# A one-core attention and gated-MLP kernel: planned idle products on TensorE, another clock model in the planner, and a table of places

## The chip, the cores and the metric

The kernel runs on one core of one Trainium2 chip. The metric is the device time of one execution in microseconds (us); of several executions the median counts. Engines: TensorE (PE, with its weight loads as PEld), VectorE (DVE), ScalarE (ACT), GpSimd (POOL) and SyncE (SP), which issues the DMAs.

## The reference, cut to what matters

Eight batches of 576 positions pass a sliding-window attention with 8 heads of 64 columns, and then a gated MLP whose gate mixes the positions. All inputs and the output are float32.

```python
scores = scale * np.matmul(q, k.transpose(0, 1, 3, 2))
bias = slopes[:, None, None] * (-np.abs(rel).astype(np.float32))[None, :, :]
mask = (rel >= 0) & (rel < window)                     # window = 128
attn = softmax(np.where(mask, scores + bias[None], -1e9))
x = np.matmul(attn, v)                                 # (8, 576, 8 * 64)
...
h = np.maximum(x @ w_in, 0.0)                          # 512 -> 1024
u, v = (h[..., :d_ff // 2], h[..., d_ff // 2:])
v_n = (v - mu) / np.sqrt(var + 1e-06)
v_s = np.einsum('ts,bsd->btd', w_spatial, v_n) + b_spatial[None, :, None]
gated = u * v_s
return (gated @ w_out).astype(np.float32)
```

## The kernel before

A batch is worked head pair by head pair (four pairs), and each pair in five tiles of one or two blocks of 64 queries (`TILES`). For a pair PE makes the scores in float32 (L635, with L634 writing the masked value), DVE adds the distance bias from a table and takes the row maximum (L667 and L774), ACT takes the exponential with its row sum (L672 and L780), and the rows are scaled (L700 on ACT or L701 on DVE; L814 and L819).

Two paths lead from there to the attention's output. The four pairs of batch 0 and the first pair of batch 1 (`RAW`) stay in float32: PE transposes the probabilities (L713, L715), they are copied out of PSUM (L382), and PE multiplies them with V (L733). All other pairs are split into two f16 halves, transposed by a DMA (L825) and multiplied with V's halves (`vh`, `vl`) on PE (L858). Outputs are split in two f16 halves again (`xt`).

When a batch has its four pairs, the gated MLP follows in units, each of them a group of 12 or 14 full-size products into one of only two PSUM banks named `m`, which ACT or DVE then empties: four units of v and one for the remaining 64 rows (L923, L945) with a layer norm each, eight of u (L974), eight that mix positions (L995, multiplied with u on DVE in L1003), eight of the output (L1023) with a DMA each.

Before all that the weights are prepared on the chip: `w_in` and `w_out` come as float64 words, which ACT and DVE turn into float32 (L398 to L414) and then, scaled by their largest magnitude, into two f16 halves (L430, L441, L456 to L461); the mixing weights are split likewise (`mixing_weights`, L530 and L534).

No order is written down. Every step is handed to a `Plan` with its engine, a weight in ns, a due value and what it reads and writes. `Plan.order` is a list scheduler in virtual time: of the steps that are ready an engine takes the one with the smallest due value. `emit` runs it forward and backward 20 times and keeps the due values of the best pass; `held` then looks for steps in the way of a waiting PE and moves one at a time, up to 100 times. Steps that name two ways (`either`) go to the engine that would end them first. Each engine's instructions are emitted in the order found, and on the chip each engine runs its own in that order. The planner's `order` also models the clock of TensorE, by the time in which PE was planned to be busy. Two kinds of products compute nothing: `warm` (L684) plans 24 groups of 5 products of 192 columns each into a bank of `x` in the first stage, and 2 more ahead of each tile's transposes in 16 tiles of batch 0.

Of the kernel before, what the change touches and what calls it, by code (L numbers as in the profile page):

```python
# [28 lines left out]

FAR = 2.0 ** 38  # L30
# [16 lines left out]
class Plan:  # L47
# [7 lines left out]
    TURN, NEAR = 95, 0  # L55
# [48 lines left out]
    def order(self, links, due, clocked):  # L104
# [9 lines left out]
        low, opened, worked = clocked, 0, 0  # L114
        while events or any(ready.values()):
# [8 lines left out]
            for e, heap in ready.items():  # L124
                if heap and free[e] <= now:
                    _, n, k = heapq.heappop(heap)
                    if e == "PE" and modes[n][head] != mode:
                        same = [x for x in heap if modes[x[1]][head] == mode and x[0] <= due[n] + self.NEAR]
                        if same:
                            heap.remove(min(same))  # L130
                            heapq.heapify(heap)
                            heapq.heappush(heap, (due[n], n, k))
                            _, n, k = min(same)
                    weight = self.ops[n][0][k][1]
                    queued[e] -= weight
                    if e == "SP":
# [35 lines left out]
    def held(self, out, due):  # L172
# [8 lines left out]
        for a, b in zip(line, line[1:]):  # L181
            idle = start[b] - end[a] + self.LAG["PE"]
            if idle < 150:
                continue
            n = b
            for _ in range(12):
                late = [(end[d], d) for d in self.ops[n][2]] + [(start[d], d) for d in self.ops[n][3]]
                if not late:
                    break
# [46 lines left out]
def attn_gmlp_kernel(ctx, tc, qk, v, w_in, w_spT, b_sp, w_out, outT):  # L236
# [3 lines left out]
    nc = tc.nc  # L240
# [908 lines left out]
```

## Time and profile before

| | |
|---|---|
| median of three executions | 577.93 us (576.01 to 578.52) |
| the profiled execution, its own time | 573.51 us |
| its span, first to last instruction | 571.8 us |
| mean granted TensorE clock | 0.991 of 2.4 GHz |
| PE, DVE, ACT busy | 549.9, 465.9, 418.9 us |
| chain that ended last, by engine | PE 68%, DVE 13%, ACT 10%, DMA 6% |

The profile shows one execution. Matmuls are pipelined and each one's record includes its latency, so the pace of PE is read from the starts of groups that follow each other and not from the length of one. An engine's busy share says little by itself: the first tenth of the span loads and prepares weights, the next builds batch 0, and from then on several batches overlap.

### The profile page before, as it was taken

What the parts mean: (1) busy time and instruction counts of PE and PEld (TensorE: products, weight loads), DVE (VectorE), ACT (ScalarE), POOL (GpSimd) and SP (SyncE); (2) the same over time, 40 slices, a digit from 0 to 9 for tenths busy, and PEclk for the clock granted to TensorE, in tenths of its full rate; (3) what the DMA queues carried; (4) which work ended last, traced back from release to release, by engine and by line L of the source; (5) the groups of instructions that cost most, each with busy time, mean ns of one, the idle gap of its engine ahead of it and who ended that gap; (6) DMA issues with size and microseconds to landing.
All of it is one profiled execution on the core that took longest, in us unless ns stands there. A gap on an engine that the chain in (4) does not pass through costs nothing.

```text
span 571.8 us, 17319 instructions
## 1 busy us (share of the span) xinstructions
PE 549.9 (96%) x6657; PEld 396.6 (69%) x6659; DVE 465.9 (81%) x1784; ACT 418.9 (73%) x1368; POOL 58.0 (10%) x121
## 2 busy tenths in 40 slices
PE   5789998999999999999999989999999999999997
PEld 4656555677667766877588765787578757785775
DVE  5889899999998689889987889969997799664541
ACT  6989999999987399589954899638983797443202
POOL 1002122100110102010111002100111010000000
PEclk9989899999999999999999999999999999999999
DMA  8951321599986686569953797737846375371002
GB/s 274 360 228 54 111 93 43 135 168 199 221 188 140 151 190 137 114 196 168 203 107 115 176 196 171 182 96 173 188 86 95 104 138 92 35 136 33 0 11 73
DMA packets 149847, 79.77 MB, mean 140 GB/s; under 512 B 129666, under 2 KB 139906, under 8 KB 149764
## 3 DMA queue, kind: packets, MB, share of 16 engines
q1 hardware_dynamic: 149764, 78.67, 59.6%
q8 instruction: 52, 0.85, 0.6%
q14 instruction: 31, 0.25, 0.1%
HBM read 37.13 MB, written 9.44 MB: 81 GB/s over the span
## 4 chain that ended last, share of the span: by engine, by line
PE 68%; DVE 13%; ACT 10%; DMA 6%; issue 2%; POOL 1%; SPq 0%; ACTq 0%; DVEq 0%; POOLq 0%
PE m L995 17%; PE m L974 13%; PE m L1023 12%; PE m L923 9%; PE s L635 6%; PE x L858 5%; DMA pt<-pq 4%; ACT prob L672 2%; DVE pq L819 2%; PE x L733 2%; ACT pq L814 2%; ACT prob L780 1%; DVE prob L774 1%; DMA out_dram<-o 1%; PE m L945 1%
## 5 line engine op out<-in xcount | busy, mean ns | idle before, releaser
L780 ACT ACTIVATE prob<-prob,stat 64x64 f32<-64x64 f32 (+1 forms) x270 | 113.2, 422 | 12.5 <-DVE stat L774 12.5
L995 PE MATMUL m<-wsp,vn 128*128 128x288 f16 x768 | 114.2, 288 | 0.3 <-ACT u L386 0.2
L1023 PE MATMUL m<-gs,wout 128*128 128x288 f16 x768 | 100.8, 286 | 0.0
L974 PE MATMUL m<-xt,win 128*128 128x288 f16 x768 | 100.4, 286 | 0.4 <-ACT vt L386 0.3
L814 ACT ACTIVATE pq<-prob,stat 64x64 f16<-64x64 f32 (+1 forms) x270 | 94.6, 421 | 6.9 <-ACT prob L780 2.6
L819 DVE SCALAR_TENSOR_TENSOR pq<-prob,stat,pq 64x64 f16<-64x64 f32 (+1 forms) x270 | 92.2, 379 | 3.6 <-ACT pq L814 3.3
L995 PEld LDWEIGHTS <-vn 128*128 128x128 f16 x768 | 74.4, 98 | 21.9 <-issue 2.9
L974 PEld LDWEIGHTS <-win 128*128 128x128 f16 x768 | 74.5, 98 | 21.4 <-issue 1.6
L1023 PEld LDWEIGHTS <-wout 128*128 128x128 f16 x768 | 73.5, 98 | 21.6 <-issue 3.3
L923 PE MATMUL m<-win,xt 128*128 128x512 f16 x384 | 86.4, 379 | 1.9 <-ACT o L1030 1.6
L774 DVE CUSTOM_DVE_ANT_0 prob<-s,tab 64x64 f32<-64x64 f32 (+1 forms) x270 | 73.1, 318 | 8.3 <-PE s L635 8.3
L923 PEld LDWEIGHTS <-xt 128*128 128x128 f16 x384 | 36.6, 98 | 46.3 <-issue 5.4
L635 PE MATMUL s<-qkraw 64*64 64x192 f32 (+2 forms) x1116 | 58.1, 321 | 5.4 <-DMA qkraw<-in_qk_dram 5.1
L1003 DVE TENSOR_TENSOR u<-m,u 128x288 f32<-128x288 f32 x64 | 29.0, 453 | 39.4 <-PE m L995 39.1
L893 POOL TENSOR_TENSOR st<-st,nhalf 128x1 f32<-128x1 f32 (+1 forms) x40 | 30.0, 752 | 304.3 <-DVE st L889 292.4
L386 ACT ACTIVATE u<-m 128x288 f32<-128x288 f32 x57 | 23.2, 407 | 51.2 <-PE m L974 51.2
L1030 ACT ACTIVATE o<-m,am 128x288 f32<-128x288 f32 x42 | 20.8, 496 | 47.3 <-PE m L1023 42.2
L635 PEld LDWEIGHTS s<-qkraw 64*64 64x64 f32 x1116 | 40.7, 135 | 15.7 <-issue 7.2
L780 ACT ACTIVATION_READ_ACCUMULATOR prob<-prob,stat 64x1 f32 (+1 forms) x270 | 51.3, 190 | 0.0
L858 PEld LDWEIGHTS <-vh 128*64 128x64 f16 x1296 | 40.0, 112 | 9.3 <-issue 9.0
L858 PE MATMUL x<-pt,vh 128*64 128x64 f16 (+1 forms) x1296 | 43.3, 205 | 0.8 <-DMA pt<-pq 0.8
L858 PE MATMUL x<-pt,vl 128*64 128x64 f16 (+1 forms) x648 | 40.1, 204 | 0.0
(157 smaller groups left out, 799.3 us busy)
## 6 DMA issues: line engine op xcount, KB each, us to landing
qkraw<-in_qk_dram SPq DMA_DIRECT2D x28, 576.0 KB, 4.0
vb<-in_v_dram SPq DMA_DIRECT2D x32, 320.0 KB, 4.1
out_dram<-o SPq DMA_DIRECT2D x64, 144.0 KB, 2.2
vn<-in_w_in_dram SPq DMA_DIRECT2D x8, 512.0 KB, 7.9
pt<-in_w_out_dram SPq DMA_DIRECT2D x4, 512.0 KB, 9.8
gw<-in_w_spT_dram SPq DMA_DIRECT2D x4, 288.0 KB, 9.2
qkraw<-in_qk_dram SPq DMA_DIRECT2D x3, 320.0 KB, 5.1
pt<-pq SPq DMA_TRANSPOSE x54, 5.2
```

What stands on the lines that cost most here:

```text
L635: nc.tensor.matmul(sc[j]()[out, at:at + k1 - k0], raw()[rows, 0, i * D:(i + 1) * D], raw()[rows, 1, k0:k1], start=True, stop=True, skip_gr ...
L774: nc.vector.tensor_tensor_reduce(pt(), sc[t][j]()[:m, SOFF[t]:SOFF[t] + n], tabs[h]()[:m, W - n:], -0.125, 3e38, ALU.add, ALU.min, st()[:m ...
L780: nc.scalar.activation(pt(), pt(), AF.Exp, bias=st()[:m, NM, j, t:t + 1], scale=-1.0, accum_out=st()[:m, SM, j, t:t + 1])
L814: nc.scalar.activation(pq[j]()[:m, 0, qs], prob[2 * (p % 2) + j]()[:m, cs], AF.Copy, scale=st()[:m, RC, j, t:t + 1])
L819: nc.vector.scalar_tensor_tensor(pq[j]()[:m, 1, qs], prob[2 * (p % 2) + j]()[:m, cs], st()[:m, RC, j, t:t + 1], pq[j]()[:m, 0, qs], ALU.mu ...
L858: nc.tensor.matmul(xp()[j * D:(j + 1) * D, x0:x0 + n * D], l()[:, kt, j * D:(j + 1) * D], rhs, start=(i > 4, j) not in seen, stop=False, s ...
L893: nc.gpsimd.tensor_tensor(st()[:m, 11:12], st()[:m, 10:11], nhalf()[:m], ALU.pow)
L923: nc.tensor.matmul(pt(), xt[c]()[:, X0[a] + t * P:X0[a] + (t + 1) * P], win()[:, c, w, DH:DF], start=(n == 0), stop=(n == 3 * NC_ - 1))
L974: nc.tensor.matmul(pt()[:, :HS], win()[:, c, w, d * P:(d + 1) * P], xt[c]()[:, X0[a] + hf * HS:X0[a] + (hf + 1) * HS], start=(n == 0), sto ...
L995: nc.tensor.matmul(pt()[:, :HS], l, r, start=(n == 0), stop=(n == len(ops) - 1))
L1003: nc.vector.tensor_tensor(u(), pt()[:, :HS], u(), ALU.mult)
L1023: nc.tensor.matmul(pt()[:, :HS], wout()[:, d, w, e * P:(e + 1) * P], gs[d]()[:, a, :], start=(n == 0), stop=(n == 3 * ND - 1))
```

## The change

The hand-placed `warm` products are removed, the 24 groups and the 16 pairs, with the bank of `x` that they held. In their place `order` works out, for each PE step that it plans after an idle stretch between 4.5 and 110 us of its virtual time, how many products of 82 ns (twice that at the lower clock) fit into the stretch, and `emit` issues so many ahead of that step (`fill`). A fill product multiplies a constant tile `ones`, widened from 128 to 192 columns, by itself and writes to a part of the last score bank that the scores leave unused: 192 columns until the first step of `products` has been issued, 64 columns after it. A fill product has no step in the plan; it stands where it was issued, ahead of its step.

The planner's clock model counts, instead of time in which PE is planned busy, a share of it that depends on the kind of step (`USE`), and other constants decide between its two levels. The preference for a step of the same array mode at equal due values goes, and so do `held` and its 100 trials. A table of 577 due values, `PLACES`, replaces the due values of these steps after the 20 passes, and one last `order` with them gives what is emitted. What the kernel computes stays, and no step is added or removed other than the idle products.

```diff
+PLACES = {
+    2: -539944.4, 5: -547637.0, 15: -535358.4, 28: -540998.3, 44: -531966.0, 46: -539701.7, 47: -546494.9, 53: -550352.7, 56: -531615.0, 68:
...
+    2901: -78795.0, 2913: -75483.7, 2914: -75481.7, 2916: -75484.7, 2922: -75483.7, 2929: -59324.7, 2933: -77043.7, 2938: -59325.7,
+}
...
-    TURN, NEAR = 95, 0
+    TURN = 95
+    USE = {"FF": 0.96, "SS": 0.88, "FX": 0.57, "XS": 0.6, "XX": 0.94}
+    FILL = 4500, 110000
...
-                    if e == "PE" and modes[n][head] != mode:
-                        same = [x for x in heap if modes[x[1]][head] == mode and x[0] <= due[n] + self.NEAR]
-                        if same:
-                            heap.remove(min(same))
-                            heapq.heapify(heap)
-                            heapq.heappush(heap, (due[n], n, k))
-                            _, n, k = min(same)
...
+                    fills = 0
...
+                            use = self.USE[modes[n]] * weight
...
-                            if now >= opened + self.CLOCK:
-                                low, worked = worked < 0.47 * self.CLOCK or low and worked < 0.85 * self.CLOCK, 0
-                                if now >= opened + 2 * self.CLOCK:
-                                    low = True
-                                opened += (now - opened) // self.CLOCK * self.CLOCK
-                            weight *= 1 + low
-                            a, z = now, now + weight
-                            while z > opened + self.CLOCK:
-                                worked += opened + self.CLOCK - a
-                                low = worked < 0.47 * self.CLOCK or low and worked < 0.85 * self.CLOCK
-                                opened += self.CLOCK
-                                a, worked = opened, 0
-                            worked += z - a
+                            idle = max(free[e], self.FILL[0])
+                            if idle < now and now < self.FILL[1]:
+                                fills = max(0, int((now - idle - 40) / (82 * (1 + low))))
+                            spans = [(free[e], idle, 0), (idle, now, fills * 80)] if idle < now else [(free[e], now, 0)]
+                            for a, z, u in spans + [(now, None, use)]:
+                                if z is None:
+                                    weight *= 1 + low
+                                    z = now + weight
+                                if a >= z:
+                                    continue
+                                u /= z - a
+                                while z > opened + self.CLOCK:
+                                    worked += (opened + self.CLOCK - a) * u
+                                    low = worked < (0.47 if low else 0.5) * self.CLOCK
+                                    opened += self.CLOCK
+                                    a, worked = opened, 0
+                                worked += (z - a) * u
                         free[e] = now + weight
                         end = free[e] + self.LAG[e]
-                    out.append((n, k, now + weight, now, at.get(n, 0), end))
+                    out.append((n, k, now + weight, now, at.get(n, 0), end, fills))
                     heapq.heappush(events, (free[e], -1))
...
-    def held(self, out, due):
-
...
-    def emit(self, passes, tries):
+    def emit(self, passes, places):
...
-        end, out, due = best
-        done = set()
-        while tries:
-            todo = [x for x in self.held(out, due) if x[1:] not in done]
-            if not todo:
-                break
...
+        due = best[1]
+        for n, t in places.items():
+            due[n] = t
+        end, out = self.order(ahead, due, True)
+        for n, k, *_, fills in out:
+            self.fill(fills)
             self.ops[n][0][k][2]()
...
-    PASSES, REPAIRS = 20, 100
+    PASSES = 20
...
-    ones = fixed([P, P], BF16, "ones")
+    ones = fixed([P, W], BF16, "ones")
...
+    def fill(n):
+        for _ in range(n):
+            if plan.begun:
+                nc.tensor.matmul(plan.kept["s"][3][:, 7 * D:], ones()[:, :P], ones()[:, :D], start=True, stop=True, skip_group_check=True)
+            else:
+                nc.tensor.matmul(plan.kept["s"][3][:, W:2 * W], ones()[:, :P], ones(), start=True, stop=True, skip_group_check=True)
+
+    plan.fill, plan.begun = fill, False
...
-    def warm(bank, n, k, due, after=()):
-
-        def f():
-            for i in range(n):
-                nc.tensor.matmul(bank()[:, :W], ones(), tabs[(k + i) % H](), start=True, stop=True)
-        plan.add("PE", n * pe(W, gap=2.5), due, f, [*after, (ones, 0)] + [(tabs[(k + i) % H], 0) for i in range(n)], [(bank, k)])
...
-        if b == 0 and t < 4:
-            warm(tp, 2, 0, due + 5000)
...
+            plan.begun = True
...
-    idle = plan.buf(ps, "x", 2, [P, 512], F32)
...
-    for k in range(16):
-        warm(idle, 5, k, -20000 + 500 * k, [(am0, ("sum", 1))])
...
-    for k in range(16, 24):
-        warm(idle, 5, k, -20000 + 500 * k, [(wv[k % 4][1], 0)])
...
-    plan.emit(PASSES, REPAIRS)
+    plan.emit(PASSES, PLACES)
```

Over the whole program PE has 235 fill products where it had 152 of `warm`: 119 of the 235 stand ahead of the first float32 transposes, the remaining 116 after them, 90 of these in six blocks of 11 to 18. Line numbers of the changed kernel are higher: L375 and L373 are the fill (192 and 64 columns), L673 and L674 the scores, L742 and L744 the transposes, L762 and L888 the two products with V, L496 and L569 the f16 halves of `w_in` and of the mixing weights on ACT, L460, L537, L633 and L643 the loads.

SP, the order of the early loads, the seventh instruction on. Before (`vn` are chunks of `w_in`, `vb` V of batch 0, `gw` the mixing weights):

```order
L421 DMA vn0_154<-in_w_in_dram 128x1024
L604 DMA vb_140<-in_v_dram 128x640
L421 DMA vn1_162<-in_w_in_dram 128x1024
L421 DMA vn2_167<-in_w_in_dram 128x1024
L421 DMA vn3_173<-in_w_in_dram 128x1024
L498 DMA gw_181<-in_w_spT_dram 128x576
L498 DMA gw_186<-in_w_spT_dram 128x576
L498 DMA gw_197<-in_w_spT_dram 128x576
L498 DMA gw_207<-in_w_spT_dram 128x576
```

SP at the same place after the change:

```order
L460 DMA vn1_154<-in_w_in_dram 128x1024
L460 DMA vn0_159<-in_w_in_dram 128x1024
L460 DMA vn2_163<-in_w_in_dram 128x1024
L643 DMA vb_140<-in_v_dram 128x640
L537 DMA gw_182<-in_w_spT_dram 128x576
L537 DMA gw_193<-in_w_spT_dram 128x576
L537 DMA gw_198<-in_w_spT_dram 128x576
L537 DMA gw_212<-in_w_spT_dram 128x576
```

The last part of V moved behind two more chunks of `w_in`, and the fourth chunk of `w_in` behind the mixing weights and one load of q and k.

ACT, where the first halves of `w_in` are made (`win`, L457; `wsp` in L530 is a mixing weight). Before, from the instruction with the fourth of the four mixing weights on:

```order
L530 ACTIVATE wsp_86<-gw_207,wam_87 128x576
L672 ACTIVATE prob2_97,rstat_103<-prob2_97,rstat_103 128x192
L457 ACTIVATE win_84<-wx_246,ham1_89 128x512
L382 COPY pq0_99<-m_686 128x256
L382 COPY pq0_99<-m_686 64x256
L457 ACTIVATE win_84<-wx_313,ham1_89 128x512
```

ACT at that place after the change, from the second of the four mixing weights on:

```order
L569 ACTIVATE wsp_86<-gw_182,wam_87 128x576
L421 CAST xt_540<-x_621 128x2x64
L711 ACTIVATE prob1_96,rstat_103<-prob1_96,rstat_103 128x192
L711 ACTIVATE prob0_95,rstat_103<-prob0_95,rstat_103 128x192
L421 COPY pq0_99<-m_636 128x256
L421 COPY pq0_99<-m_636 64x256
L496 ACTIVATE win_84<-wx_273,ham1_89 128x512
L496 ACTIVATE win_84<-wx_278,ham1_89 128x512
```

Two of the four mixing weights moved behind the halves of `w_in`, which the first unit of v needs.

PE, the end of one group and the start of the scores of a later pair (`s`), in the stage in which batches overlap. Before:

```order
L995 LDWEIGHTS vn_2857
L995 MATMUL m<-wsp,vn_2857 128x288
L635 MATMUL s_69<-qkraw 64x64
L635 MATMUL s_66<-qkraw 64x64
L634 LDWEIGHTS ones
L634 MATMUL s_69<-masked,ones 64x64
```

PE at such a place after the change:

```order
L888 LDWEIGHTS vl
L888 MATMUL x<-pt,vl 64x64
L674 MATMUL s_69<-qkraw 64x64
L674 MATMUL s_66<-qkraw 64x64
L673 LDWEIGHTS ones
L673 MATMUL s_69<-masked,ones 64x64
```

Scores stood right behind the products with V of another pair at two places of the program before, and stand so at seven now. Counted from the first mixing unit (L995) to the end, PE goes from a group of full-size products to scores, to products with V or to the unit of the remaining rows 50 times before and 41 times after.

PE, a tile of batch 0 in the float32 path. Before, with two idle products (L688) into the bank of the transposes:

```order
L715 MATMUL m_686<-ident_71,prob1_96 64x128
L688 LDWEIGHTS ones_72
L688 MATMUL m_704<-tab0_76,ones_72 128x192
L688 LDWEIGHTS ones_72
L688 MATMUL m_704<-tab1_77,ones_72 128x192
L713 MATMUL m_704<-ident_71,prob0_95 128x128
```

After, with one fill product (L375), into the score bank:

```order
L674 MATMUL s2_68<-pt_132 64x192
L674 MATMUL s3_69<-pt_132 64x192
L375 LDWEIGHTS ones_72
L375 MATMUL s3_69<-ones_72 128x192
L762 MATMUL x_558<-pq0_99,vb_140 64x64 x2
L742 MATMUL m_561<-ident_71,prob2_97 128x128
```

The idle products left the place ahead of the transposes and stand ahead of whichever step the plan has waiting.

## Rows read from the trace of the kernel before

**Rows 1.** The page, parts 1 and 2: busy time, share and instructions of three engines, and the granted clock in 40 slices of 14.3 us, in tenths of full speed.

```profile
PE 549.9 (96%) x6657; PEld 396.6 (69%) x6659; DVE 465.9 (81%) x1784; ACT 418.9 (73%) x1368; POOL 58.0 (10%) x121
...
PEclk9989899999999999999999999999999999999999
```

**Rows 2.** The windows of the stages: start and end in us, length, then busy us and instructions of each engine, the granted clock as a share of full speed, the DMA engines' mean share and GB/s.

```profile
0.00:36.00 36.00, 24.87 (x249) 18.88 (x249) 26.47 (x122) 28.69 (x82) 4.78 (x15) 0.97 0.95 336
36.00:99.00 63.00, 58.77 (x651) 36.61 (x650) 58.47 (x203) 60.57 (x187) 11.20 (x20) 0.96 0.22 72
99.00:165.00 66.00, 64.98 (x936) 45.91 (x934) 63.43 (x279) 62.92 (x222) 6.75 (x17) 0.98 0.90 189
165.00:500.00 335.00, 333.24 (x4138) 244.98 (x4135) 285.16 (x1105) 246.09 (x836) 32.46 (x64) 1.00 0.66 140
500.00:568.40 68.40, 68.05 (x693) 50.19 (x692) 32.36 (x81) 20.10 (x45) 2.77 (x5) 1.00 0.21 49
```

**Rows 3.** The waits of PE up to 99 us, the one ahead of the last float32 transposes: the engine, tile and line that waited, what ended the wait, us in total, times, longest us.

```profile
PE s L713 <- ACT prob L700: 2.0, 2, 1.7
```

**Rows 4.** ACT's groups of instructions by line and shape, up to 140 us: busy us and mean ns of one behind the first bar, idle us ahead of them behind the second.

```profile
L700 ACT ACTIVATE prob<-prob,rstat 128x192 f32<-128x192 f32 x28 | 12.0, 460 | 0.5 <-DVE rstat L679 0.5
L430 ACT ACTIVATE ab<-wx 128x512 bf16<-128x512 f32 x12 | 7.3, 633 | 0.9 <-DVE wx L414 0.8
...
L382 ACT CAST xt<-x 128x128 f16<-128x128 f32 x17 | 4.4, 261 | 0.8 <-PE x L733 0.6
L457 ACT ACTIVATE win<-wx,ham 128x512 f16<-128x512 f32 x5 | 3.5, 723 | 0.0
...
L841 ACT ACTIVATE vh<-vb,am 128x640 f16<-128x640 f32 x3 | 2.5, 822 | 0.0
...
L382 ACT COPY pq<-m 64x128 f32<-64x128 f32 x2 | 0.4, 258 | 0.7 <-PE m L715 0.7
L382 ACT CAST xt<-x 128x64 f16<-128x64 f32 x1 | 0.2, 212 | 0.0
```

**Rows 5.** DVE's groups by line and shape, up to 140 us, with the same columns.

```profile
L774 DVE CUSTOM_DVE_ANT_0 prob<-s,tab 128x192 f32<-128x192 f32 x34 | 10.4, 343 | 0.0
...
L414 DVE SCALAR_TENSOR_TENSOR wx<-vn,wx 128x512 uint32<-128x512 uint32 x8 | 5.5, 682 | 0.0
L410 DVE SCALAR_TENSOR_TENSOR wx<-vn,wx 128x512 int32<-128x512 int32 x8 | 5.5, 682 | 0.0
...
L701 DVE TENSOR_SCALAR prob<-prob,rstat 128x192 f32<-128x192 f32 x12 | 3.5, 315 | 0.1
...
L845 DVE SCALAR_TENSOR_TENSOR vl<-vb,am,vh 128x640 f16<-128x640 f32 x3 | 2.6, 866 | 0.0
```

**Rows 6.** The timeline of PE, groups by their start and length in us, at three places in which groups follow each other without idle time.

```profile
123.32 1.63 PE L1023 MATMUL m<-gs,wout 128*128 128x288 f16 x12
124.79 0.53 PE L995 MATMUL m<-wsp,vn 128*128 128x288 f16 x3
...
126.51 1.63 PE L1023 MATMUL m<-gs,wout 128*128 128x288 f16 x12
128.07 0.50 PE L635 MATMUL s<-qkraw 64*64 64x64 f32 x6
...
200.75 0.30 PE L858 MATMUL x<-pt,vh 128*64 128x128 f16 x4
...
202.30 0.50 PE L635 MATMUL s<-qkraw 64*64 64x64 f32 x6
...
264.64 0.30 PE L858 MATMUL x<-pt,vh 128*64 128x128 f16 x4
...
266.19 3.11 PE L1023 MATMUL m<-gs,wout 128*128 128x288 f16 x24
```

**Rows 7.** The chain that ended last, in order of time: start and length in us; the first mixing unit and a later one.

```profile
99.20 3.14 PE m L995 x14
...
189.73 1.82 PE m L995 x14
```

**Rows 8.** Windows of 3 us, with the columns of rows 2: two of those in which the lower clock was granted.

```profile
69.00:72.00 3.00, 3.00 (x40) 1.75 (x40) 2.37 (x7) 2.77 (x9) 1.57 (x2) 0.64 0.00 0
...
99.00:102.00 3.00, 3.00 (x17) 1.87 (x14) 2.32 (x15) 3.00 (x12) 0.00 (x0) 0.52 0.00 0
```

**Rows 9.** All waits of PE from 99 us on, with the columns of rows 3.

```profile
PE m L923 <- ACT o L1030: 1.6, 1, 1.6
PE x L858 <- DMA pt<-pq: 0.8, 2, 0.5
PE m L974 <- ACT vt L386: 0.3, 1, 0.3
PE m L995 <- ACT u L386: 0.2, 1, 0.2
```

**Rows 10.** The timeline of PE at 21 us: a block of 40 products of `warm`, and what starts behind it.

```profile
20.82 3.47 PE L688 MATMUL x<-tab,ones 128*128 128x192 bf16 x40
24.13 0.65 PE L441 MATMUL m<-wsp,ones 128*128 128x288 bf16 x4
```

More of the change, by code (lines that the diff above doesn't have):

```diff
@@ L102, in links, with order @@
         return after, left
-    def order(self, links, due, clocked):
+    def order(self, links, due, clocked, phase=0):
         head, rear = (0, 1) if clocked else (1, 0)
@@ L113, in order @@
         out, queued, now, dma, at = [], dict.fromkeys(self.LAG, 0), 0, 0, {}
[L114 removed]
+        low, opened, worked = clocked, -phase, 0
         while events or any(ready.values()):
@@ L170, in order @@
         return now, out
-    def held(self, out, due):
-        start, end, ready, engine, lines, spot = {}, {}, {}, {}, {e: [] for e in self.LAG}, {}
-        for n, k, _, now, at, fin in out:
-            e = self.ops[n][0][k][0]
-            start[n], end[n], ready[n], engine[n], spot[n] = now, fin, at, e, len(lines[e])
-            lines[e].append(n)
-        found = []
-        line = lines["PE"]
[L181 to L188, printed above, removed]
-                    break
-                t, n = max(late)
-                if ready[n] + 40 < start[n]:
-                    first = spot[n]
-                    row = lines[engine[n]]
-                    while first and start[row[first - 1]] >= ready[n]:
-                        first -= 1
-                    if first < spot[n]:
-                        found.append((idle, n, row[first]))
-                    if first:
-                        n = row[first - 1] if first == spot[n] else n
-        found.sort(key=lambda x: -x[0])
-        return found
-    def emit(self, passes, tries):
+    def emit(self, passes, places):
         ahead, behind = self.links(False), self.links(True)
@@ L210, in emit @@
             if best is None or end < best[0]:
-                best = end, out, list(due)
+                best = end, list(due)
             for n, _, t, *_ in out:
@@ L215, in emit @@
                 due[n] = -t
-        end, out, due = best
-        done = set()
-        while tries:
-            todo = [x for x in self.held(out, due) if x[1:] not in done]
-            if not todo:
-                break
-            _, n, x = todo[0]
-            done.add((n, x))
-            new = list(due)
-            new[n] = due[x] - 1
-            tries -= 1
-            e, o = self.order(ahead, new, True)
-            if e < end:
-                end, out, due = e, o, new
-        for n, k, *_ in out:
+        due = best[1]
[4 more added lines that the diff above has]
+            self.fill(fills)
             self.ops[n][0][k][2]()
@@ L440, in f @@
                 for c, (ap, a, z) in enumerate(rows):
-                    nc.tensor.matmul(pt()[:, :step], ones()[a:z], ap()[a:z, h * step:(h + 1) * step], start=c == 0, stop=c == len(rows) - 1)
+                    nc.tensor.matmul(pt()[:, :step], ones()[a:z, :P], ap()[a:z, h * step:(h + 1) * step], start=c == 0, stop=c == len(rows) - 1)
         plan.add("PE", len(pts) * len(rows) * pe(step, gap=3), due, f, keys + [(ones, 0)], [(pt, 0) for pt in pts])
@@ L561, in largest @@
             plan.add("DVE", 350, due, f, keys + [(ident, 0)], [(am, 7), (wide, 0)])
-            plan.add("PE", pe(P), due + 1, lambda: nc.tensor.matmul(pt()[:, :P], ones(), wide()[:, 0, :], start=True, stop=True),
+            plan.add("PE", pe(P), due + 1, lambda: nc.tensor.matmul(pt()[:, :P], ones()[:, :P], wide()[:, 0, :], start=True, stop=True),
                      [(wide, 0), (ones, 0)], [(pt, 0)])
```

64 rows, old and new, of the table PLACES are left out of this document.

## The prediction

> **What bounds the kernel now.** I read the windows by stage first [rows 2], since the shares of the whole span [rows 1] mix stages with different limits. Up to 36 us the DMA engines are at 0.95: the loads set the pace. From 36 to 99 us ACT is busy 60.57 of 63 us, DVE and PE 58.5 and 58.8: batch 0 and the weights go through ACT and DVE, and PE waits for them, as it does for 1.7 us ahead of the last float32 transposes [rows 3]. From 99 us, where the first mixing unit starts, PE is busy 64.98 of 66, 333.24 of 335 and 68.05 of 68.4 us, and its groups start at the pace of their columns [rows 6]. So the end is set by three things: when the first mixing unit starts, how much PE work lies behind it, and what PE loses there. The work behind it is 469 us (99.2 to 568.4), almost the same in both orders: up to the first mixing unit the changed order has the same units of v and u, transposes and products with V, and 8 small score products more.
>
> **The change part by part.**
>
> *a. Start of the first mixing unit.* It hangs on what ACT and DVE do ahead of it. On ACT I count in the order what stands ahead of the first exponential of the later pairs (L780), which follows right behind it. Fewer now: two scalings of V (L841), three scalings of probabilities (L700), one magnitude (L430), two copies to `xt`: 2 x 0.822 + 3 x 0.460 + 0.633 + 2 x 0.261 = 4.18 us. More: one half of `w_in` (L457), three copies out of PSUM, two short ones to `xt`: 0.723 + 3 x 0.258 + 2 x 0.212 = 1.92 us. Net -2.3 us [rows 4]. On DVE, ahead of its first product of u with a mixing result, the largest kinds are: two word operations of one weight chunk (2 x 0.682) and one remainder of V (0.866) fewer, three distance biases (3 x 0.343) and three scalings (3 x 0.315) more, net -0.3 us [rows 5]. So the first mixing unit comes 0.3 to 2.3 us earlier if idle time stays as it is. I take -1.5, nearer to ACT's number, since ACT is the fuller of the two [rows 2]. The early loads are shuffled too: the last part of V lands behind two more chunks of weights, and two of the mixing weights' steps move behind `w_in`'s. The cover for both is that V's scaled values and the mixing weights are used long after the first unit of v. If the cover fails, the price is idle ACT time in the stage up to 36 us, where 7.3 us of it are free already.
>
> *b. Leaving full-size groups.* An output unit of 12 takes 1.47 us to the start of the next mixing unit and 1.56 us if scores follow: 0.09 us for leaving [rows 6]. Scores right behind products with V cost nothing: 202.30 - 200.75 = 1.55 us, as 266.19 - 264.64 ahead of an output unit. Behind the first mixing unit there are 50 such changes before and 41 now: 9 x 0.09 = -0.8 us, on the path, since PE is the bound there. This term has little spread.
>
> *c. The clock at the first mixing unit.* It took 3.14 us where a later one takes 1.82 [rows 7], at a granted clock of 0.52 [rows 8], so mostly at 1.2 GHz. Two other low stretches lie where ACT is the bound (the one at 69 us is shown), and I count nothing for them. If the six `fill` products now ahead of the scores before this unit, and the 17 ahead of the units of u, hold the clock, -1.3 us; else 0. Between these I take -1.3: in the window ahead of the drop at 99 us PE idled behind the wait of 1.7 us [rows 3], and this kind of idle time is what now gets products.
>
> *d. Waits of PE behind 99 us.* They add up to 1.6 + 0.8 + 0.3 + 0.2 = 2.9 us [rows 9]. All of them are the work of a particular order: a bank that ACT empties late, a DMA transpose that lands late. A new order removes these and may bring others. Nothing in the rows says which, so the bounds are -2.9 and +3 (as many again). Counted in the order at the paces of the groups [rows 6], the scores of a pair stand at least 20 us of PE work ahead of its products with V now, and 18 at the closest before. That speaks for fewer late transposes. I take -1.5, half of it.
>
> *e. The fills themselves.* One costs 83 ns at 2.4 GHz: (24.13 - 20.82) / 40 [rows 10]. The 119 early ones replace 120 of `warm` in a stage that the DMA bounds. The other 116 are 9.6 us of PE, where 32 of `warm` were 2.7. PE idles 4.2 us between 36 and 99 [rows 2] and some 3 more before that, so they fit only just, if the plan is right about when each step becomes ready. They sit in PE's own queue: whatever stands behind a block waits for it to the end, and so do DVE and ACT, which empty PE's banks. A fill also waits until DVE has read the scores out of its bank. I take 0, since PE is not the bound up to 99 us, with 0 and +7.5 as bounds (the six long blocks, 90 x 0.083).
>
> *Sum.* -1.5 - 0.8 - 1.3 - 1.5 = -5.1 us. The profiled execution took 573.51 us, so the sum gives 568.4 for one like it. But the three timed ones have their median 4.4 us above it. The profile shows what one low stretch on the path costs, 1.3 us, and 4.4 us are about three of them. That the other executions met more low stretches is an estimate from these rows and is not shown. If the fills act as in c, they take away part of that: I take half, -2.2 us. 577.93 - 5.1 - 2.2 = 570.6, say 570.5 us.
>
> **The rivals.**
>
> *The clock holds everywhere:* the whole 4.4 us goes, not half: 577.93 - 5.1 - 4.4 = 568.4, down to 564 if a and d reach their good ends (-0.8 - 1.4) and the ACT idle time of 2.4 us between 36 and 99 goes as well [rows 2]. For it: the spread of the four executions, 573.5 to 578.5 us. Against it: no row shows the other three.
>
> *The clock is not in the plan's hands:* the low stretches come at other places than the planner thinks, c and the 2.2 us do not come: 577.93 - 3.8 = 574.1 us. For it: the planner's model starts at the same state in each pass, and the four executions of one program differ by 5 us. The Trainium skill (TensorE: Matmul & The Clock Gate, in "What's actually happening") says that the hardware's look at PE's activity does not reset when a kernel starts; by that rule an order tuned to one start would lose terms of the kind of c in other executions, which is this rival's time. The trace of one execution neither bears it out nor speaks against it.
>
> *New waits for old ones:* every unit of the gated MLP needs one of two banks that ACT or DVE empties, and the planner's durations differ from the chip's. Three waits like that of 1.6 us [rows 9] eat the sum: 577.93 - 5.1 + 4.8 = 577.6 us, no change.
>
> *The fills hold PE up (slower):* where the plan has a step ready later than the chip has it, its block of fills stands in front of it. With ACT busy 60.57 of 63 us [rows 2], time that its input is held for is lost. If all six long blocks do so it is +7.5, and with only b left 577.93 + 7.5 - 0.8 = 584.6 us. It passes the bound of 0.5% (580.8 us) from half of these blocks on. Against it: the plan was made with durations under which PE's groups after 99 us leave hardly a wait, so its idea of readiness can't be far off.
>
> *The change does nothing:* the stretches that PE idles in are not those of the plan. Then b alone is left, 577.1 us; I count it with the new waits.
>
> **How the numbers follow.** Forecast 0.42, the clock holds everywhere 0.18, the clock is not in the plan's hands 0.15, new waits 0.15, fills hold PE up 0.10. The forecast's own range is 566 (a and d at their good ends, -0.8 - 1.4, and all of the 4.4) to 575 (a at -0.3, c and d at 0). The range of 8 in 10 reaches from 563.5, just under the end of the good rival, to 577, the forecast without c, d and the executions' share and with a at 0; it leaves out the slower case and part of the new waits. About 0.5% is what a measurement can tell from no change here: below 575.0 us counts as faster, above 580.8 as slower. Faster: 0.41 + 0.18 + 0.10 + 0.02 = 0.71. Slower: 0.10. The same: 0.19.
>
> **What would show it.** For a, the first group of the mixing units starts at 97 to 99 us. For b, groups of an output unit ahead of scores still take 1.56 us, and there are 41 of these changes. For c, no granted clock below 1 between 25 and 110 us, and a first mixing unit of 1.7 to 1.8 us. For d, the waits of PE behind the first mixing unit add up to under 2.9 us. For e, no PE step is released by a fill, and no instruction that DVE or ACT wait for starts right at the end of a block. The prediction is wrong if the first mixing unit starts after 99 us, which would mean that the fills or the moved loads hold up the first stages, or if new waits of over 3 us show behind it.

## The result, and the profile after

The changed kernel took 567.75 us (median of four runs, 567.62 to 567.81), the kernel before, measured beside it, 577.03 us (576.01 to 578.52). The ratio is 0.9837, with a 95% interval of 0.981 to 0.9863: 9.3 us faster. The forecast was 570.5 us with a range of 563.5 to 577. The profiled execution took 567.71 us with a span of 566.0 us; that of before took 573.51 us with a span of 571.8 us. So 5.8 of the 9.3 us can be looked for in two traces, and 3.5 us lie between the profiled execution of before and the median of the others.

Parts 1 and 2 of the page of the changed kernel, the lines that answer to [rows 1]: PE is as busy as before, and the granted clock has no slice under nine tenths.

```profile
PE 550.2 (97%) x6739; PEld 401.4 (71%) x6742; DVE 464.3 (82%) x1778; ACT 418.3 (74%) x1374; POOL 57.3 (10%) x121
...
PEclk9999999999999999999999999999999999999999
```

The windows of the changed kernel, cut and read as in [rows 2]:

```profile
0.00:36.00 36.00, 27.12 (x291) 20.14 (x291) 26.53 (x126) 27.90 (x85) 4.76 (x15) 1.00 0.95 332
36.00:99.00 63.00, 62.47 (x730) 42.09 (x729) 59.96 (x215) 62.01 (x194) 8.96 (x20) 1.00 0.26 81
99.00:165.00 66.00, 65.22 (x941) 47.12 (x941) 65.09 (x268) 64.02 (x225) 8.48 (x17) 1.00 0.82 188
165.00:500.00 335.00, 333.71 (x4263) 247.26 (x4262) 287.72 (x1113) 248.63 (x842) 32.34 (x64) 1.00 0.68 143
500.00:568.40 68.40, 61.73 (x525) 44.75 (x522) 24.99 (x60) 15.71 (x32) 2.77 (x5) 0.99 0.10 34
```

Three things are to be seen. The clock column is at 1.00 where it was 0.96 to 0.98 up to 165 us. From 36 to 99 us ACT idles 63 - 62.01 = 1.0 us, where it idled 2.4. And in the last window PE is busy 61.73 us where it was 68.05, since it ends earlier.

The timeline of PE of the changed kernel (start and length in us) at the first mixing unit, in place of [rows 7]. The first row is the block of six fills ahead of it.

```profile
94.74 0.35 PE L373 MATMUL s<-ones 128*128 128x64 bf16 x6
95.02 1.28 PE L674 MATMUL s<-qkraw 64*64 64x192 f32 x16
96.23 0.54 PE L1025 MATMUL m<-wsp,vn 128*128 128x288 f16 x3
96.61 0.41 PE L1025 MATMUL m<-r,l 128*128 128x288 f16 x2
96.85 1.27 PE L1025 MATMUL m<-wsp,vn 128*128 128x288 f16 x9
97.95 1.63 PE L1004 MATMUL m<-xt,win 128*128 128x288 f16 x12
```

The unit starts at 96.23 us and the next work at 97.95, 1.72 us later. In the trace of before it started at 99.13 us and took 3.14 [rows 7]. The timeline of PE before:

```profile
99.13 0.90 PE L995 MATMUL m<-wsp,vn 128*128 128x288 f16 x3
```

So 2.9 us come from the start and about 1.4 from the clock. The waits of PE from 96 us on (columns of [rows 3], in place of [rows 9]) add up to 2.0 us where they were 2.9. Of the four of before two are gone (1.6 and 0.2 us) and two have another size (the late transposes, 0.8 before and 0.4 now, and the units of u behind `vt`, 0.3 and 0.5):

```profile
PE m L1004 <- ACT vt L425: 0.5, 2, 0.3
PE x L888 <- DMA pt<-pq: 0.4, 1, 0.4
PE m L953 <- ACT vt L425: 0.4, 1, 0.4
PE m L1053 <- ACT wout L529: 0.3, 1, 0.3
PE m L1025 <- DVE u L1033: 0.2, 1, 0.2
PE m L975 <- DVE o L1061: 0.2, 1, 0.2
```

Leaving full-size groups costs what it did. The timeline of PE, two such units of 12 in the changed kernel:

```profile
107.20 1.63 PE L1004 MATMUL m<-xt,win 128*128 128x288 f16 x12
108.76 0.88 PE L674 MATMUL s<-qkraw 64*64 64x192 f32 x16
...
111.30 1.63 PE L1004 MATMUL m<-xt,win 128*128 128x288 f16 x12
112.77 0.53 PE L1025 MATMUL m<-wsp,vn 128*128 128x288 f16 x3
```

It is 108.76 - 107.20 = 1.56 us ahead of scores and 112.77 - 111.30 = 1.47 ahead of a mixing unit, the two numbers of [rows 6]. Counted in the trace there are 42 such changes behind the first mixing unit (50 before).

The end of PE's work, in the timelines before and after:

```profile
566.73 1.63 PE L1023 MATMUL m<-gs,wout 128*128 128x288 f16 x12
```

```profile
554.76 7.27 PE L1053 MATMUL m<-gs,wout 128*128 128x288 f16 x58
```

From the start of the first mixing unit to the end of PE's last product it is 568.36 - 99.13 = 469.23 us before and 562.03 - 96.23 = 465.80 after, 3.4 less. Of these, 1.4 are the clock's and 0.7 the eight changes'. About 1.0 belongs to sixteen score products of 192 columns that went ahead of the unit (216 score products stand there where 200 did; eight take 0.49 us, 27.99 to 28.48 us in a timeline under "Later fills alone"). What is left over for the waits is 0.3, where the rows of waits give 0.9. From PE's last product to the end of the span it takes 0.6 us more than before. Together: 2.9 + 3.4 - 0.6 = 5.7 us, and the spans differ by 5.8.

### The profile page after: what moved, and what is told of

It reads as the page before. It is cut to its first block, busy times and chain, and to the rows that moved or that the text cites. A ratio compares the mean times of both kernels' runs of the same rounds, so it can differ in the third digit from the quotient of the medians.

```text
span 566.0 us, 17497 instructions
## 1 busy us (share of the span) xinstructions
PE 550.2 (97%) x6739; PEld 401.4 (71%) x6742; DVE 464.3 (82%) x1778; ACT 418.3 (74%) x1374; POOL 57.3 (10%) x121
## 4 chain that ended last, share of the span: by engine, by line
PE 64%; ACT 18%; DVE 10%; DMA 4%; issue 2%; POOL 0%; SPq 0%; ACTq 0%; DVEq 0%
PE m L1025 17%; PE m L1004 14%; PE m L1053 11%; PE m L953 7%; PE s L674 5%; PE x L888 5%; ACT prob L810 4%; ACT pq L844 3%; DMA pt<-pq 3%; PE s L375 2%; ACT prob L711 2%; DVE pq L849 2%; ACT junk L646 2%; DVE prob L804 1%; DMA out_dram<-o 1%
## 5 line engine op out<-in xcount | busy, mean ns | idle before, releaser
L810 ACT ACTIVATE prob<-prob,stat 128x192 f32<-128x192 f32 (+1 forms) x270 | 113.9, 426 | 13.2 <-DVE stat L804 12.8
L1025 PE MATMUL m<-wsp,vn 128*128 128x288 f16 x768 | 112.8, 286 | 0.2 <-DVE u L1033 0.2
L844 ACT ACTIVATE pq<-prob,stat 64x64 f16<-64x64 f32 (+1 forms) x270 | 96.6, 425 | 8.0 <-DMA pt<-pq 4.0
L1004 PE MATMUL m<-xt,win 128*128 128x288 f16 x768 | 100.2, 286 | 0.6 <-ACT vt L425 0.5
L804 DVE CUSTOM_DVE_ANT_0 prob<-s,tab 128x192 f32<-128x192 f32 (+1 forms) x270 | 75.6, 317 | 5.1 <-PE s L674 4.9
L923 POOL TENSOR_TENSOR st<-st,nhalf 128x1 f32<-128x1 f32 (+1 forms) x40 | 27.2, 683 | 339.6 <-DVE st L919 334.7
L674 PE MATMUL s<-qkraw 64*64 64x192 f32 (+1 forms) x1116 | 57.1, 318 | 4.3 <-DMA qkraw<-in_qk_dram 4.3
L810 ACT ACTIVATION_READ_ACCUMULATOR prob<-prob,stat 128x1 f32 (+1 forms) x270 | 52.0, 193 | 0.0
L674 PEld LDWEIGHTS s<-qkraw 64*64 64x64 f32 x1116 | 40.4, 134 | 13.0 <-issue 5.2
L888 PEld LDWEIGHTS <-vh 128*64 128x64 f16 x1296 | 40.2, 112 | 8.2 <-issue 6.3
L888 PE MATMUL x<-pt,vh 128*64 128x64 f16 (+1 forms) x1296 | 43.2, 204 | 0.5 <-DMA pt<-pq 0.4
L888 PE MATMUL x<-pt,vl 128*64 128x64 f16 (+1 forms) x648 | 40.1, 204 | 0.0
```

Of the source, the lines that this page charges most:

```text
L674: nc.tensor.matmul(sc[j]()[out, at:at + k1 - k0], raw()[rows, 0, i * D:(i + 1) * D], raw()[rows, 1, k0:k1], start=True, stop=True, skip_gr ...
L804: nc.vector.tensor_tensor_reduce(pt(), sc[t][j]()[:m, SOFF[t]:SOFF[t] + n], tabs[h]()[:m, W - n:], -0.125, 3e38, ALU.add, ALU.min, st()[:m ...
L810: nc.scalar.activation(pt(), pt(), AF.Exp, bias=st()[:m, NM, j, t:t + 1], scale=-1.0, accum_out=st()[:m, SM, j, t:t + 1])
L844: nc.scalar.activation(pq[j]()[:m, 0, qs], prob[2 * (p % 2) + j]()[:m, cs], AF.Copy, scale=st()[:m, RC, j, t:t + 1])
L888: nc.tensor.matmul(xp()[j * D:(j + 1) * D, x0:x0 + n * D], l()[:, kt, j * D:(j + 1) * D], rhs, start=(i > 4, j) not in seen, stop=False, s ...
L923: nc.gpsimd.tensor_tensor(st()[:m, 11:12], st()[:m, 10:11], nhalf()[:m], ALU.pow)
```

## The experiments

Two questions were asked. Does the gain come through the granted clock or through the order (the first four)? And do idle products in PE's queue hold up work that is ready (the other eight)? Each ratio is to runs of the kernel before on the same chip, with medians of 577.17 us for the first four, 577.29 for the next four and 578.61 for the last four. "Clock" is the mean granted clock of an execution; what lies ahead of its first change on record counts as full speed in it, which hides the slow start of two runs below. Gains in us are differences of medians; where the ratio gives another, both are said.

**The kernel before, again.** No edit.

> The kernel before, unchanged, to see time and granted clock of several executions side by side. Theory K (the clock): the executions differ by how many low stretches of the clock they meet, so a longer one has a lower mean granted clock, and 0.003 less (one stretch of 3.4 us at half of the 571.8 us span) goes with 1.3 us more; the median of 577 us should show a mean clock of about 0.98. Theory O (the order): the executions differ for other reasons, and clock and time are unrelated.

577.0 us (573.22 to 581.46, ten runs), ratio 0.9992 (0.9955 to 1.003). Most of the spread is not noise: over the 29 runs of before that the first four share, the time goes with the clock (correlation -0.87), by 0.34 us for each 0.001 (0.40 and 0.54 in the other two groups of runs). At 0.971 they took 581.1 us on average (two runs), at 0.976 579.1 (six), at 0.982 576.1 (five), at 0.985 576.4 (ten), at 0.991 573.4 (one). That is theory K, but not all of it is the clock: the ten at 0.985 go from 574.6 to 577.7 us. Two profiles of this program show the difference: from 25 to 36 us the granted clock is 0.89 in the first and 0.57 in this one, and the first mixing unit starts at 99.13 and at 100.61 us. The median clock is 0.982. The profiled execution of before, at 0.991, was one of the best.

**The order of before with fills.** Fills are put where the plan of before leaves PE idle (155 of them); `warm` and the order stay.

```diff
-        for n, k, *_ in out:
+        free = 0
+        for n, k, fin, now, *_ in out:
+            if self.ops[n][0][k][0] == "PE":
+                idle = max(free, 4500)
+                if idle < now < 110000:
+                    self.fill(max(0, int((now - idle - 40) / 82)))
+                free = fin
...
```

The dots stand for lines that define `fill` as in the change and widen `ones`.

> The order of before with its products of warm kept, and fill products added in the stretches that its own plan leaves idle (155 more products). Theory K: the clock stays at 0.996 or above and the time falls by the clock's part, 1.3 us of the first mixing unit and 3.5 us of the timed executions, to about 572 us, with a spread under 0.5 us. Theory O: the order is unchanged, so 577 us, or more by what the added products hold up.

573.22 us (571.61 to 574.04, ten runs), ratio 0.9929 (0.9905 to 0.9953), and every run had a clock of 0.999 or 1.0. So fills alone hold the clock and gain 4.0 us. By the slope above, 0.018 of clock would be worth 6; whether the difference is what these 155 products cost, or work that the clock does not speed up, was not taken apart. At a full clock the ten runs still spread over 2.4 us, where under 0.5 was expected. The first mixing unit starts at 100.82 us, not earlier than in the two profiles of before.

**The table without fills.** `warm` is gone too in this one, as in the change.

```diff
         for n, k, *_, fills in out:
-            self.fill(fills)
             self.ops[n][0][k][2]()
```

> The changed kernel's order with its table, but no fill product is issued. Theory K: the low stretches come back, also in the first 25 us, which no warm products fill now: clock 0.98 or less, first mixing unit at 98 us or later, 573 us or more. Theory O: the order makes the gain, 568 to 569 us.

572.79 us (569.43 to 573.99, eight runs), ratio 0.991 (0.9878 to 0.9942): 4.4 us faster than before (5.2 by the ratio), close to theory K's 573. Its time too goes with the clock: 569.4 us at 0.997 (two runs), 572.6 to 573.1 at 0.994, 573.4 and 574.0 at 0.991. These means are too good, since PE is at the lower clock up to about 35 us here too, ahead of the first change on record (eight scores at 34.19 us take 0.92 us; see "Later fills alone"). The first mixing unit starts 4 us later than with the fills, though the order is the same. The timeline of PE:

```profile
100.22 0.54 PE L1024 MATMUL m<-wsp,vn 128*128 128x288 f16 x3
...
101.94 1.64 PE L1003 MATMUL m<-xt,win 128*128 128x288 f16 x12
```

**Fills without the table.** The plan of the passes alone, with its own 228 fills.

```diff
-    plan.emit(PASSES, PLACES)
+    plan.emit(PASSES, {})
```

> The changed kernel with an empty table: fills and clock model stay, the due values are those of the 20 passes alone, without the 100 trials of before. Theory K: most of the gain stays, 571 to 573 us at a clock of 0.996 or above. Theory O: the gain is the table's, so 576 us or more although the clock is full.

581.01 us (576.82 to 584.09, ten runs), ratio 1.0072 (1.0038 to 1.0107): slower than before. The granted clock of its page, over slices of 14.4 us, and the windows of the low part:

```profile
PEclk9779999999999999999999999999999999999999
```

```profile
14.00:30.00 16.00, 11.82 (x97) 9.55 (x96) 12.65 (x40) 13.76 (x35) 1.03 (x2) 0.78 0.98 330
30.00:40.00 10.00, 9.95 (x82) 6.83 (x82) 6.96 (x38) 6.57 (x22) 0.53 (x2) 0.67 0.83 329
```

So fills do not hold the clock in every order: theory O's time came, but at a clock of 0.982 to 0.991. No run has this plan without its fills, so the loss can be the plan's alone. The first mixing unit starts at 103.76 us, and PE's waits behind it add up to 6.9 us (3.6 in the kernel before, again), two for ACT's output copies among them, 2.3 us together.

**Early fills alone.** The 119 ahead of 25 us in the plan stay.

```diff
-        for n, k, *_, fills in out:
-            self.fill(fills)
+        for n, k, _, now, *_, fills in out:
+            self.fill(fills if now < 25000 else 0)
```

> The changed kernel with the 119 fill products of the first 25 us alone; the 116 later ones are not issued. Theory K (fills pay through the granted clock alone): the clock is full from 11 us on, then some low stretches return between 30 and 100 us, mean clock about 0.994, 2 us over the 567.75 of the whole change: 570. Theory Q (products in PE's queue hold real work up, so fewer are better): 566 to 567 us.

571.18 us (569.22 to 576.19, ten runs), ratio 0.9911 (0.9878 to 0.9944), at a median clock of 0.991. The first mixing unit starts at 98.09 us. The order with as many early products as before had gains 6.1 us (5.1 by the ratio), near to theory K; the other 2.3 to 3.4 us, to the two medians of the changed kernel (568.85 and 567.75), need the later fills, with which the clock is 0.996 and more.

**Later fills alone.** As above, with `now >= 25000` (116 fills).

> The changed kernel with the 116 later fill products alone. Theory K: the lower clock lasts until the first real products run in a row, at 25 to 35 us, and PE's work there, though the loads bound that stage, comes later: 569 to 571 us, with a full clock behind. Theory Q, for the first stage: it is bound by the loads, so its products pay nothing, and 567.7 us stays.

572.74 us (570.81 to 575.9, eight runs), ratio 0.9954 (0.9914 to 0.9994): no better than no fills at all, and above what either theory gave. The clock column has no record ahead of its first change and shows 1.00, but the lengths tell. The timeline of PE in this run:

```profile
25.84 1.14 PE L480 MATMUL m<-wsp,ones 128*128 128x288 bf16 x4
...
27.61 0.92 PE L674 MATMUL s<-qkraw 64*64 64x192 f32 x8
...
34.62 0.92 PE L674 MATMUL s<-qkraw 64*64 64x192 f32 x8
...
36.31 0.56 PE L674 MATMUL s<-pt 64*64 64x192 f32 x8
```

And the same groups in the changed kernel:

```profile
25.80 0.66 PE L480 MATMUL m<-wsp,ones 128*128 128x288 bf16 x4
...
27.99 0.56 PE L674 MATMUL s<-qkraw 64*64 64x192 f32 x8
28.48 0.41 PE L744 MATMUL m<-ident,prob 64*64 64x64 f32 x4
```

Eight score products take 0.92 us up to 35 us and 0.56 from 36 us on: without early idle products PE is at the lower clock in each group of the loading stage that can be compared. From 27 us on, when the real work comes, it hands ACT its inputs late: ACT is busy 24.82 us up to 36 us, with all fills 27.90. Those 3 us are not caught up with (ACT is busy 61.56 of the 63 us behind); the first mixing unit starts at 99.98 us, and at 98.09 with the early fills alone. So the two kinds need each other: beside the order without fills (572.79 us) the early ones alone gain 1.6 us by the medians and nothing by the ratios, the later ones alone nothing by either, both together 3.9 to 5.0 us. Why the later ones pay only behind the early ones is argued here from ACT's lost 3 us; no run shows it by itself.

**Half more later fills.** The later blocks are made 1.5 times as long (170 products).

```diff
+            self.fill(int(1.5 * fills) if now >= 25000 else fills)
```

> The changed kernel with every later block of fill products half as long again (170 instead of 116, 54 more, 4.5 us of PE). Theory K: PE is not the bound before the first mixing unit, so under 1 us is added: 568 to 568.7. Theory Q: the products stand in front of steps that are ready, and most of the 4.5 us is added: 571 to 572.

572.59 us (571.0 to 573.94, nine runs), ratio 0.9927 (0.9904 to 0.9951), at clocks of 0.996 to 1.0. That is 3.7 to 4.8 us over the two medians of the change (568.85 and 567.75), for at most 54 x 0.083 = 4.5 us of PE work more, as theory Q had it. The timeline of PE at the last long block, and at the first mixing unit:

```profile
84.32 2.24 PE L375 MATMUL s<-ones 128*128 128x192 bf16 x25
86.39 3.10 PE L1004 MATMUL m<-xt,win 128*128 128x288 f16 x24
...
99.18 0.54 PE L1025 MATMUL m<-wsp,vn 128*128 128x288 f16 x3
```

In the changed kernel the block starts at 81.31 us and the unit at 96.23, so 3 us of it are there already.

**Fills with the planner's trials in place of the table.** The function `held` and its loop of 100 trials come back, on the plan with the new clock model.

```diff
...
-    plan.emit(PASSES, PLACES)
+    plan.emit(PASSES, 100)
```

> The changed kernel with its fills and clock model, but the order refined by the 100 trials of before in place of the table. If the table only replaces what the trials did, 568 to 570 us. If the table finds more than the trials (what the 581.0 us with neither leaves room for), 573 to 578 us, with a clock under 0.996 as in that run.

579.82 us (575.3 to 583.57, ten runs), ratio 1.0049 (1.0016 to 1.0082): slower than either case, so the table does more than the trials did. The first mixing unit starts at 104.19 us, and the clock is low at 16, 30 and 341 us.

**A quarter less of the later fills.** `int(0.75 * fills)` for those behind 25 us (81 products).

> The changed kernel with every later block of fill products a quarter shorter (81 instead of 116, 2.9 us of PE less). If the products hold up steps that are ready one for one on this side too, as half as many again did (4.5 us of products, 4.8 us more), 565 us at a full clock. If the blocks of the change fit their stretches, PE only idles longer: 567.75 us at a full clock, or 569 to 571 where low stretches return.

567.13 us (566.7 to 567.86, four runs), ratio 0.9835 (0.9782 to 0.9888), at clocks of 0.997 to 1.0: 1.7 us under the changed kernel beside it (the next one), with ranges that touch, and 0.6 under its first median. So fewer products hold the clock as well, but the 565 us of the first case did not come.

**The changed kernel again,** beside the last three edits.

> The changed kernel once more, beside the others of this call: 567.6 to 567.8 us as in its first four executions, clock 0.996 or above.

568.85 us (567.81 to 569.16, four runs), ratio 0.986 (0.9807 to 0.9914), at clocks of 0.996 to 1.0. That is 1.1 us over its first median, and outside what was expected, so a difference of 1 us between groups of runs says little. In its profile the granted clock is low from 15 to 18 us (0.87 on average from 12 to 25), and the first mixing unit starts at 96.19 us all the same: no cost of this stretch is seen.

**Narrow later fills.** The 116 have 64 columns (eight of them had so before, the other 108 had 192).

```diff
-    def fill(n):
+    def fill(n, wide):
...
-            if plan.begun:
+            if plan.begun or not wide:
```

> The changed kernel with the same 116 later products, but of 64 columns in place of 192, so that they take about a third of PE's time. Theory K: PE streams less in the waiting stretches, low stretches come back, clock about 0.991 as without these products: 571 us. Theory Q: PE is held up less and the clock holds: 563 to 566 us.

567.99 us (566.67 to 568.7, four runs), ratio 0.9841 (0.9777 to 0.9906), at clocks of 0.996 to 0.999. The time is between the two theories. A third of the columns at the same places hold the clock behind the early fills as well, up to the first mixing unit (95.61 us). Its profile shows one low stretch, at 325 us, where no fills stand.

**The long blocks alone.** Of the later fills the six long blocks stay (90 products), the short ones (26) go.

```diff
+            self.fill(fills if now < 25000 or fills > 10 else 0)
```

> The changed kernel with the six long later blocks (90 products) and none of the short ones (26 products, 2 us). If the long ones hold the clock, 567 to 568 us at 0.996 or above; if each block is needed where it stands, 569 to 571 us.

565.98 us (565.42 to 566.58, four runs), ratio 0.9814 (0.9761 to 0.9867). It is 2.9 us (0.5%) under the changed kernel beside it, and their four runs each lie apart. It is better than either case that was expected, and the best version, on four runs. PE's timeline at its first mixing unit:

```profile
93.61 1.06 PE L674 MATMUL s<-qkraw 64*64 64x128 f32 x16
95.03 0.87 PE L674 MATMUL s<-qkraw 64*64 64x192 f32 x14 [0.36 <-ACT pq L421]
95.84 0.54 PE L1025 MATMUL m<-wsp,vn 128*128 128x288 f16 x3
...
97.56 1.63 PE L1004 MATMUL m<-xt,win 128*128 128x288 f16 x12
```

Where six fills stood, PE now idles 0.36 us, and the unit still takes 97.56 - 95.84 = 1.72 us: these six were not what held the clock.

## Why the prediction was right, and where it was not

The sign and the time were right (567.75 in 563.5 to 577, 2.75 us under the forecast), and the two causes that it named, the order and the clock, are both there. Both single runs show it: fills without the new order gain 4.0 us, the new order without any idle product 4.4, both together 9.3 (4.1, 5.2 and 9.4 by the ratios). The forecast started from 577.93 us, where the kernel before now took 577.03, so the gain is further from it than the time: 9.3 us for 7.4.

*a, the start of the first mixing unit,* was mis-sized: -2.9 us, taken as -1.5 with an end at -2.3. Up to the unit ACT is busy 28.69 + 60.70 = 89.4 us before and 27.90 + 59.37 = 87.3 after, so 2.1 of the 2.9 are less ACT work, near to the 2.3 that were counted; moving from there toward DVE's -0.3 was the mistake. The other 0.8 are idle time of ACT, which the step took as unchanged. What that assumption hid is shown by the order run at four states of PE. With all fills the unit starts at 96.2 us, with the early ones alone at 98.1, with the later ones alone at 100.0, with none at 100.2. The ACT work that the order saves is a gain only where PE delivers in time. The step also has one number wrong: not 8 but 16 more score products stand ahead of the unit, about 1.0 us of PE's work behind it, which "almost the same in both orders" left out.

*b, leaving full-size groups,* held: 42 where 41 were counted, at 0.09 us, -0.7 us. No run undid this part alone, so its size rests on the paces.

*c, the clock at the first mixing unit,* came out in size: 1.72 us, and no granted clock below 1 between 25 and 110 us. But the reason given was not it, and that the -1.3 came is in part luck: without the six fills ahead of it the unit takes the same 1.72 us, and in the profile of the table without any fills it takes 1.72 as well (100.22 to 101.94), with low clocks at 38 and 69 us instead. What the fills change is how much of the whole is at the lower clock, not this one unit; which block holds which stretch was not taken apart.

*d, the waits behind,* was mis-sized: -0.3 to -0.9 us for -1.5. Two waits of before are gone, two have another size and four are new, none over 0.5 us in total. To that extent the rival of new waits for old ones came true, far from its price of 4.8. These sums change by up to 0.7 us from one execution to the next (3.6 and 2.3 us in the second profiles of the two kernels), so the size is no better known than that.

*e, the fills themselves.* "No PE step is released by a fill" was wrong. In the chain that ended last of the changed kernel (start and length in us) three of the long blocks stand, and the longest of the early ones:

```profile
20.06 4.87 PE s L375 x59
...
34.20 1.24 PE s L375 x15
...
41.24 1.59 PE s L375 x18
...
46.56 1.26 PE s L375 x14
```

A chain is inferred, but the run with half more of the later ones confirms that these stand at the edge: 4.5 us more of products cost 3.7 to 4.8 us. Fewer gain less evenly: a quarter less 1.7 us for 35 x 0.083 = 2.9 us of products, the 26 short ones 2.9 us for at most 26 x 0.083 = 2.2, so that something else changes with them. Against the first median of the change these are 0.6 and 1.8 us. So the fills as planned cost some 1 to 3 us that they need not, where the step took 0 with bounds of 0 and 7.5. The rival in which the fills hold PE up had the mechanism, and lost because what they give is more: without the later ones it is 571.18 us.

*The share of the executions* was mis-sized, in the good direction: 3.5 us where half of 4.4 was taken. The changed kernel's profiled execution lies at its median (567.71 and 567.75 us), so the whole of the gap is gone. What was an estimate is now shown: the runs of before differ for the most part by their clock, and the profiled one was among the best. From a median clock of 0.982 to 0.996 and more it is 14 x 0.34 = 4.8 us or more by the slope, an estimate; the forecast had 1.3 + 2.2 = 3.5 us for the clock. The rest of the 9.3 us, some 4, is the order's by this estimate, for which a, b and d had 3.8; but the fills on the old order gave 4.0 for a larger step of the clock, and the start of the first mixing unit belongs to both.

*The clock is not in the plan's hands* was the rival at 574.1 us. For this order it is refuted: the eight executions of the changed kernel had clocks of 0.996 to 1.0 and stayed within 567.62 to 569.16 us. The reason given for it, that the look at PE's activity does not reset when a kernel starts (the Trainium skill, TensorE: Matmul & The Clock Gate, in "What's actually happening"), agrees with the kernel before, whose one program met clocks of 0.971 to 0.991. No run shows the start of that look; what the runs show is that this order with its fills stayed at 0.996 or above in all eight. For the plan without the table the rival is not refuted: with its 228 fills the clock was 0.982 to 0.991.

*The clock holds everywhere* (568.4 us, 0.18) is the case that came closest.

*Still open:* why the plans without the table meet low clocks at 16 and 30 us in spite of their fills (a short one at 15 us the changed kernel met too, without a loss that is seen); how many of the 119 early products are needed, since no run took fewer of them than all or none; whether narrow fills are better than wide ones (567.99 against 568.85 us, ranges that overlap); and whether the 2.9 us of the long blocks alone come again in more runs than four.

## What to carry to other kernels

Before a sum is set against a median, look at the mean granted clock of all executions: here 0.001 of it was 0.34 us or more, and the profiled one was among the best. Idle products paid here where PE waits in the stages that feed another engine, since the slow clock delayed that engine's inputs (ACT busy 24.82 us instead of 27.90), and half as many again cost about their full length; so try fewer of them too, the short blocks first. An order and its idle products belong together: either alone gave about half of the gain, and a plan without the table was slower than before in spite of its 228 fills (581.01 us).

## What was not expected of the hardware

Without early idle products PE worked at the lower clock up to about 35 us in each group that can be compared (table without fills, later fills alone). In the latter it was busy for 7.00 of the 7 us from 27 to 34, with float32 scores, transposes and products with V among a few fills, and eight scores still took 0.92 us at 34.62, and 0.56 us from 36 us on. The window (columns of [rows 2]; its clock of 1.00 stands ahead of the first record):

```profile
27.00:34.00 7.00, 7.00 (x47) 3.96 (x48) 2.81 (x11) 2.22 (x10) 0.53 (x2) 1.00 1.02 393
```

And fills of 64 columns kept the clock as high as fills of 192 at the same places (0.996 to 0.999 against 0.996 to 1.0).
